# Output pairs in pieces of 6, 12 and 6 slots, with bank changes at the score matmuls

## The chip, the cores and the metric

The kernel runs on one core of a Trainium2 chip. The metric is device time in microseconds (us) of one execution. Below, TensorE is PE, VectorE DVE, ScalarE ACT, GpSimd POOL, and SyncE's DMA queue SP.

## What is computed

For x of 2048 tokens by 576 features, a gated mix of softmax attention (32 heads of 18 features) and an MLP with layer norm (576 to 4608 to 576), all in float32:

```python
def _A_ref(x, wqkv, wo):                 # attention, H = 32, Dh = 18
    q, k, v = qkv[0], qkv[1], qkv[2]
    scores = jnp.einsum("bhqd,bhkd->bhqk", q, k) * scale
    p = _softmax(scores, axis=-1)
    o = jnp.einsum("bhqk,bhkd->bhqd", p, v)
    return (...).reshape(B, S, D) @ wo
def _B_ref(x, w1, b1, w2, b2):
    y = _layernorm(x, axis=-1)
    h = _gelu(jnp.einsum("bsd,df->bsf", y, w1) + b1)
    return jnp.einsum("bsf,fd->bsd", h, w2) + b2
g = _sigmoid((x * gate_w).sum(-1, keepdims=True))
return g * a + (1 - g) * b
```

## The kernel before

Numbers keep float32's precision by being split: a value is a rounded high part plus a low part, and a product is three matmuls (high by high, high by low, low by high).

**The attention loop** (lines 1026 to 1057) has 512 steps: 32 units (a pair of heads, half of the queries) of 16 key chunks. A step has two *score pairs*, `s2` (line 236): two matmuls, one for each head, on row halves 0 to 63 and 64 to 127 of the array. Both write one PSUM tile of two banks, `pss`, of which there is only one, and one exponential on ScalarE (line 238) empties it. So a score pair waits for the exponential of the pair before. In each even step the values' products `pv` (line 253) of two steps follow the first score pair. Two *rounds* a step, `s1_round` (line 195), compute the raw scores of a later unit for their maximum; each is two matmuls with a reduction on DVE for each (line 197), and they share three PSUM banks, so the second matmul of a round reuses the bank of the first matmul of the round before.

**The MLP** fills the time between score pairs. `mlp` is a generator; `fill` takes one piece from it, up to the next cut. It is called three times in two steps: after the even step (share 0), between the two score pairs of the odd step (share 1) and after the odd step (share 2). So two steps make a period with four intervals between score pairs: the first holds `pv`, the others the pieces of share 0, 1 and 2. The MLP's unit of work is a *slot*: two matmuls side by side, one on each row half.

- `h_pair` (line 433): two hidden tiles of 128 by 512, 27 slots of 512 columns. ScalarE then adds the bias (Identity), squares and takes a Tanh (lines 454, 486, 484); GpSimd does the GELU's other steps and the split. It takes one period with pieces of 9 slots, or two with 4, 5, 5 and 4, 5, 4.
- `out_pair` (line 513): 128 tokens by 576 outputs of four hidden tiles, 24 slots of 288 columns: four tiles, in the order `ORDER = (0, 1, 3, 2)`, three products each, and two turns. In turn 0 row half h writes bank h; in turn 1 it writes the other bank. The two halves must not write one bank at a time, so a drain of TensorE stands between the turns (line 502), after 12 slots. Pieces end after 7 and 15 slots. DVE then adds both banks to the sum (line 522).

A group of hidden tiles (36 of them) is an `h_pair` over two periods, four output pairs of one period each, and an `h_pair` over one period: seven periods, 14 steps. The order of every engine's queue is fixed by this program; waits between engines are semaphores. In the first nine groups the MLP's weights are also split: ScalarE copies the high part (line 349), GpSimd subtracts (through line 154), and `ready` (line 366) does that at once when a matmul needs a weight that is not yet prepared.

Of the kernel before, what the change touches and what calls it, by code (L numbers as in the profile page):

```python
# [27 lines left out]
G = 4  # L28
NFC = F // P
NG = NFC // G  # L30
ND = 288
SCALE = DH ** -0.5
GC1 = 0.7978845608028654 * 0.044715
GC0 = 1.0 / 0.044715
LN_EPS = 1e-5
# [23 lines left out]
def gated_mix_kernel(ctx: ExitStack, tc: tile.TileContext, x, wqkv, wo, w1, b1, w2, b2, gate_w, out):  # L59
# [121 lines left out]
        nc.sync.dma_start(VT[pair % 2], v_scr[:, :, pair, :].rearrange("k p e -> p k e"))  # L181

    M4 = {}

    def s1_round(u, r):


        t, kb = (r % 8, r // 8) if u == 0 else divmod(r, 4)
        if r == 0:
            M4[u] = asm.tile([P, 2, 8, 4], F32, name="m4")  # L190
        qa, ka = QA[u % 3], KA[u // 2 % 2]
        for h in range(2):
            r0 = 64 * h
            ps = psum(ps_s1)
            nc.tensor.matmul(ps, qa[r0:r0 + 54, t * P:(t + 1) * P], ka[r0:r0 + 54, kb * TB:(kb + 1) * TB],  # L195
                             start=True, stop=True)
            nc.vector.tensor_reduce(M4[u][:, h, t, kb:kb + 1], ps, axis=AX.X, op=ALU.max)  # L197

# [29 lines left out]
    def s2(u, kc, qb):  # L228
        qa, ka = QA[u % 3], KA[u // 2 % 2]
        n = u * NT + kc  # L230
        if n < 2 and qb == 0:
            RING.insert(n, pp.tile([P, 2, 2, TB], F32, name="p"))
        ps = ps_s2.tile([P, 2, TB], F32, name="pss")
        for h in range(2):
            r0 = 64 * h
            nc.tensor.matmul(ps[:, h, :], ka[r0:r0 + 56, kc * P:(kc + 1) * P], qa[r0:r0 + 56, qb * TB:(qb + 1) * TB],  # L236
                             start=True, stop=True)
        nc.scalar.activation(RING[n % 3][:, qb], ps, AF.Exp, scale=SCALE)  # L238

# [60 lines left out]
    def mlp():  # L300
# [190 lines left out]
        def out_pair(i, t, acc):  # L491

            tb, g = seq[i]
            tok = slice(t * P, (t + 1) * P)
            cs = [slice(nn * ND, (nn + 1) * ND) for nn in range(2)]
            ps = [psum(ps_w) for _ in range(2)]
            ends = {7, 15} if piece[0] == 0 else cuts(24, (3, 2, 1)[piece[0]])
            k = 0
            for turn in range(2):
                if turn == 1:  # L500

                    nc.tensor.drain()
                for j in ORDER:
                    while (i, j) not in HT:
                        cut[0] = 3
                        yield 0
                    hh, hl = HT[i, j]
                    w_ = ready(W2, (i * (G // 2) + j // 2, j % 2))
                    for h_, p_ in ((hh, 0), (hh, 1), (hl, 0)):
                        for h in (0, 1) if turn == 0 else (1, 0):  # L510
                            r = slice(64 * h, 64 * h + 64)
                            nn = h ^ turn
                            nc.tensor.matmul(ps[nn][:, :ND], h_[r, tok], w_[p_][r, cs[nn]],  # L513
                                             start=(k == 0), stop=(k == 6 * G - 1))
                        k += 1
                        if k < 6 * G:
                            if k in ends:
                                cut[0] = 1
                            yield 131
            for nn in range(2):  # L520
                dst = acc[:, t, cs[nn]]
                nc.vector.scalar_tensor_tensor(dst, ps[nn][:, :ND], 0.5, b2b[:, cs[nn]] if g == 0 else dst,  # L522
                                               op0=ALU.mult, op1=ALU.add)
            if g == NG - 1:
                tt = tb * 4 + t
                nc.gpsimd.tensor_scalar(acc[:, t, :], acc[:, t, :], gate1[:, tt:tt + 1], 1.0, op0=ALU.mult, op1=ALU.mult)
                defer(12 if tb < NB - 1 else 4, lambda: nc.sync.dma_start(b_scr[tt * P:(tt + 1) * P, :], acc[:, t, :]))
            cut[0] = 2
            yield 131
# [496 lines left out]
    for u in range(NU):  # L1026
        for kc in range(NT):
            step = u * NT + kc
            if kc == 1:
                if u + 2 < NU:  # L1030
                    load_q(u + 2)
                if u % 2 == 0 and u // 2 + 1 < NPAIR:
                    load_k(u // 2 + 1)
                    load_v(u // 2 + 1)
            if step in (NSTEP - NT, NSTEP - NT + 1, NSTEP - NT + 2, NSTEP - NORM):
                assert hidden[0] == NB - 1
                next(proj)


            next_round()  # L1040
            s2(u, kc, 0)
            run_due(462.0)
            if kc % 2:
                fill(step, 1)
            elif step > 0:
                pv(step - 2)
                while ROWS:
                    ROWS.pop(0)()
                run_due(2080.0)
            if kc % 2:  # L1050
                next_round()
            s2(u, kc, 1)
            if kc % 2 == 0:

                next_round()
            run_due(462.0)
            fill(step, 2 if kc % 2 else 0)
    pv(NSTEP - 2)
# [29 lines left out]
```

## Time and profile before

| | |
|---|---|
| runs, us | 2430.2, 2429.12, 2428.8 (median 2429.12) |
| span of the profiled execution, us | 2421.7 |
| chain that ended last | PE 87%, DVE 3%, issue 3%, POOL 2%, DMA 2%, ACT 2% |
| L513 output pairs, share of that chain | 20% |
| L253, L433, L236, L195, shares of that chain | 19%, 17%, 12%, 10% |
| DMA, mean GB/s | 136 |

The profile shows one execution from its first to its last instruction; of that execution it gives the span alone, and the runs' times include what lies around it. A row of the timeline has the start, the length of a merged run of equal instructions, the engine, the line, the tiles, the shapes and the count; in brackets stands the idle time of the engine before it and what ended that. PEld are TensorE's weight loads, which run ahead of its matmuls. A row of the waits has who waited for whom, the sum in us, how many times and the longest. A row of stretches has the busy time and the count of instructions for PE, PEld, DVE, ACT and POOL, then the granted TensorE clock (1.00 is full), the DMA share and GB/s.

### The profile page before, as it was taken

Reading aid. Unit: us, or ns where it says so; the run is one execution under the profiler, and the core shown is the slowest. Engines: PE = TensorE matmul, PEld = TensorE weight load, DVE = VectorE, ACT = ScalarE, POOL = GpSimd, SP = SyncE. Lnnn points to the kernel's source line nnn. Section 1 sums busy time; section 2 is a strip of 40 time slices with the busy share of each in tenths; the row PEclk is TensorE's granted clock in tenths of the full one; section 3 lists DMA queues with packets and bytes.
Section 4 is the critical chain, followed back from the end, with each engine's and each line's share of the span. In section 5 each row is a group of like instructions: output and inputs, shape, how many; then the busy total and the mean of one; then the engine's idle time right before and its main releaser. Section 6 shows DMA issues by size and latency. Waiting matters only on the chain.

```text
span 2421.7 us, 50623 instructions
## 1 busy us (share of the span) xinstructions
PE 2331.6 (96%) x20585; PEld 1622.0 (67%) x20585; DVE 1652.3 (68%) x2890; ACT 1364.2 (56%) x1604; POOL 965.2 (40%) x964
## 2 busy tenths in 40 slices
PE   8998899998999999999999999999999999999978
PEld 7876556665666666666666666666666666666638
DVE  4665566666667777777777777777777777777415
ACT  4222566655656666666665666666655566666551
POOL 3001565555555444433343444444344334444400
PEclk9999999999999999999999999999999999999979
DMA  7647944434356443333254423242354243232146
GB/s 235 234 150 208 266 143 116 155 113 134 126 159 161 144 149 97 109 103 104 88 157 156 152 95 116 92 133 92 114 160 149 92 144 112 86 120 85 61 144 205
DMA packets 164639, 330.40 MB, mean 136 GB/s; under 512 B 57742, under 2 KB 84402, under 8 KB 153570
## 3 DMA queue, kind: packets, MB, share of 16 engines
q1 hardware_dynamic: 161414, 321.71, 42.5%
q10 hardware_dynamic: 2992, 5.46, 0.6%
q8 instruction: 162, 2.65, 0.5%
q14 instruction: 71, 0.58, 0.1%
HBM read 234.31 MB, written 96.73 MB: 137 GB/s over the span
## 4 chain that ended last, share of the span: by engine, by line
PE 87%; DVE 3%; issue 3%; POOL 2%; DMA 2%; ACT 2%; SPq 0%; ACTq 0%; POOLq 0%; DVEq 0%
PE ps L513 20%; PE ps L253 19%; PE ps L433 17%; PE pss L236 12%; PE ps L195 10%; PE ps L749 4%; PE ps L767 2%; PE ps L988 2%; POOL zz L154 1%; ACT p L238 1%; DVE m L197 1%; DMA big<-y_scr 1%; POOL w L154 1%; PE ps L673 1%; DVE p L733 0%
## 5 line engine op out<-in xcount | busy, mean ns | idle before, releaser
L197 DVE TENSOR_REDUCE m<-ps 128x1 f32<-128x512 f32 x2048 | 1298.5, 684 | 478.1 <-PE ps L195 477.2
L238 ACT ACTIVATE p<-pss 128x1024 f32<-128x1024 f32 x684 | 701.6, 1026 | 507.0 <-PE pss L236 495.2
L513 PE MATMUL ps<-w,hh 64*128 64x288 f32 x4352 | 506.4, 303 | 37.0 <-POOL w L154 20.8
L154 POOL TENSOR_SCALAR zz<-zz 128x512 f32<-128x512 f32 x288 | 178.7, 621 | 872.6 <-ACT zz L486 726.5
L433 PE MATMUL ps<-big,w 64*128 64x512 f32 x3888 | 517.3, 392 | 4.4 <-DMA big<-y_scr 4.3
L236 PE MATMUL pss<-qa,ka 56*128 56x512 f32 x2048 | 483.0, 439 | 20.7 <-ACT p L238 12.3
L238 ACT ACTIVATE ring<-pss 128x1024 f32<-128x1024 f32 x340 | 348.7, 1026 | 248.9 <-PE pss L236 244.3
L513 PEld LDWEIGHTS ps<-w,hh 64*128 64x128 f32 x4352 | 404.6, 189 | 99.0 <-issue 46.1
L195 PE MATMUL ps<-ka,qa 54*128 54x512 f32 x2048 | 458.9, 411 | 7.3 <-DVE m L197 3.6
L433 PEld LDWEIGHTS ps<-big,w 64*128 64x128 f32 x3888 | 389.0, 185 | 73.1 <-DMA big<-y_scr 5.7
L236 PEld LDWEIGHTS pss<-qa,ka 56*128 56x128 f32 x2048 | 199.5, 187 | 275.4 <-ACT p L238 125.6
L154 POOL TENSOR_TENSOR zz<-zz,z 128x512 f32<-128x512 f32 x288 | 371.4, 1290 | 24.0
L513 PE MATMUL ps<-w,hl 64*128 64x288 f32 x2176 | 352.9, 296 | 0.0
L253 PE MATMUL ps<-p,vt 128*32 128x512 f32 x2736 | 348.6, 604 | 0.0
L195 PEld LDWEIGHTS ps<-ka,qa 54*128 54x128 f32 x2048 | 239.4, 186 | 38.8 <-DVE m L197 14.0
L513 PEld LDWEIGHTS ps<-w,hl 64*128 64x128 f32 x2176 | 237.6, 189 | 0.3 <-POOL hl L154 0.2
L154 POOL TENSOR_TENSOR w<-x,w 128x576 fp32r<-128x576 f32 (+1 forms) x54 | 98.2, 1835 | 332.3 <-ACT w L349 308.0
L154 POOL TENSOR_TENSOR hl<-zz,hh 128x512 fp32r<-128x512 f32 x136 | 177.0, 1301 | 11.4
L253 PE MATMUL ps<-ring,vt 128*32 128x512 f32 x1360 | 181.3, 605 | 0.0
L253 PEld LDWEIGHTS ps<-p,vt 128*32 128x32 f32 x2736 | 71.9, 110 | 151.6 <-issue 150.4
L522 DVE SCALAR_TENSOR_TENSOR x<-ps,x 128x288 f32<-128x288 f32 x256 | 105.0, 452 | 38.3 <-PE ps L513 25.9
L749 PE MATMUL ps<-big,wqk 128*128 128x512 f32 x504 | 127.0, 406 | 0.9 <-DVE wqk L667 0.7
(93 smaller groups left out, 1341.8 us busy)
## 6 DMA issues: line engine op xcount, KB each, us to landing
w<-w_scr SPq DMA_DIRECT2D x54, 1152.0 KB
w<-w_scr SPq DMA_DIRECT2D x108, 576.0 KB
x<-in_B_w_dram SPq DMA_DIRECT2D x72, 288.0 KB
w_scr<-w SPq DMA_DIRECT2D x18, 1152.0 KB
w_scr<-w SPq DMA_DIRECT2D x36, 576.0 KB
big<-y_scr SPq DMA_DIRECT2D x42, 384.0 KB
qa<-qk_scr SPq DMA_DIRECT2D x192, 72.0 KB
ka<-qk_scr SPq DMA_DIRECT2D x90, 144.0 KB
```

The lines of the kernel that those rows point to most:

```text
L154: fn(*args, **kw)
L195: nc.tensor.matmul(ps, qa[r0:r0 + 54, t * P:(t + 1) * P], ka[r0:r0 + 54, kb * TB:(kb + 1) * TB], start=True, stop=True)
L197: nc.vector.tensor_reduce(M4[u][:, h, t, kb:kb + 1], ps, axis=AX.X, op=ALU.max)
L236: nc.tensor.matmul(ps[:, h, :], ka[r0:r0 + 56, kc * P:(kc + 1) * P], qa[r0:r0 + 56, qb * TB:(qb + 1) * TB], start=True, stop=True)
L238: nc.scalar.activation(RING[n % 3][:, qb], ps, AF.Exp, scale=SCALE)
L253: nc.tensor.matmul(OB[u][r:r + 32, :], v[:, k, 19 * h:19 * h + 32], RING[c % 3][:, qb, h, :], start=(k == 0), stop=(k == NT - 1))
L433: nc.tensor.matmul(ps[h], wt[w_][r, c, :], Y[s_][r, c, :], start=(k == 0), stop=(k == 26))
L513: nc.tensor.matmul(ps[nn][:, :ND], h_[r, tok], w_[p_][r, cs[nn]], start=(k == 0), stop=(k == 6 * G - 1))
L522: nc.vector.scalar_tensor_tensor(dst, ps[nn][:, :ND], 0.5, b2b[:, cs[nn]] if g == 0 else dst, op0=ALU.mult, op1=ALU.add)
L749: nc.tensor.matmul(ps, w_[:, c, ms], big[:, s_, :], start=(k == 0), stop=(k == len(prods) - 1))
L767: nc.tensor.matmul(ps[:, :ND], big[:, s_, tok], w_[:, c, cs], start=(k == 0), stop=False)
L988: nc.tensor.matmul(ps[:, :ND], OT[b][2][:, s_, tok], w_part(w_, c)[:, cs], start=(k == 0), stop=(k == 13))
```

## The change

An output pair that starts in a piece of share 0 is cut into three parts: 6 slots of turn 0 (the first two tiles), all 12 of turn 1, then the other 6 of turn 0. Each part is one piece, so a bank change falls on the place between two pieces, where score matmuls stand. A pair that starts elsewhere has 12 and 12. Where score matmuls were issued since the last slot, the drain is replaced by an order: an instruction without work on ScalarE waits for the part's last matmul, and the next part's first matmul waits for that instruction. Where none were issued, the drain stays. In the odd step the round ahead of the second score pair now follows it, as in the even step.

```diff
     def s1_round(u, r):
...
+        parted[0] += 1
         for h in range(2):
...
         ps = ps_s2.tile([P, 2, TB], F32, name="pss")
+        parted[0] += 1
...
-            ends = {7, 15} if piece[0] == 0 else cuts(24, (3, 2, 1)[piece[0]])
+            prods = [(j, s_, p_) for j in ORDER for s_, p_ in ((0, 0), (0, 1), (1, 0))]
+            if piece[0] == 0:
+
+                parts = (prods[:6], 0), (prods, 1), (prods[6:], 0)
+            else:
+                parts = (prods, 0), (prods, 1)
             k = 0
-            for turn in range(2):
-                if turn == 1:
+            for place, (part, turn) in enumerate(parts):
+                fresh = place and parted[0] > since
+                if place and not fresh:
 
                     nc.tensor.drain()
-                for j in ORDER:
+                for x_, (j, s_, p_) in enumerate(part):
                     while (i, j) not in HT:
                         cut[0] = 3
                         yield 0
-                    hh, hl = HT[i, j]
+                    h_ = HT[i, j][s_]
                     w_ = ready(W2, (i * (G // 2) + j // 2, j % 2))
-                    for h_, p_ in ((hh, 0), (hh, 1), (hl, 0)):
...
+                    for h in range(2):
+                        r = slice(64 * h, 64 * h + 64)
+                        nn = h ^ turn
+                        mm = nc.tensor.matmul(ps[nn][:, :ND], h_[r, tok], w_[p_][r, cs[nn]],
+                                              start=(k == 0), stop=(k == 6 * G - 1))
+                        if fresh:
+                            tc.add_manual_dep(mm.ins, told.ins.name, SYNC, reason="other rows' bank")
+                            fresh = False
+                    since = parted[0]
+                    if place < len(parts) - 1 and x_ + 1 == len(part):
+                        told = nc.scalar.nop()
+                        tc.add_manual_dep(told.ins, mm.ins.name, SYNC, reason="this row's last")
+                    k += 1
+                    if k < 6 * G:
+                        if x_ + 1 == len(part) and piece[0] < 2:
+                            cut[0] = 1
+                        yield 131
...
-            if kc % 2:
-                next_round()
             s2(u, kc, 1)
-            if kc % 2 == 0:
-
-                next_round()
+            next_round()
             run_due(462.0)
```

TensorE's order in a regular period of an output pair, before, from the round ahead of the odd step's first score pair to its second score pair (L195 is a round, L236 a score pair, L513 slots; `hh` and `hl` are the hidden tile's high and low parts; two matmuls are a slot; drains are not listed):

```order
L195 MATMUL ps<-ka_107,qa_104 128x512 [waits DVE_49] x2
L236 MATMUL pss<-qa_105,ka_106 128x512 [waits Activation_49]
L236 MATMUL pss<-qa_105,ka_106 128x512
L513 MATMUL ps<-w_20123,hh 128x288 x2
L513 MATMUL ps<-w_20123,hl 128x288 x2
L513 MATMUL ps<-w_20121,hh 128x288 x4
L513 MATMUL ps<-w_20121,hl 128x288 x2
L513 MATMUL ps<-w_20117,hh 128x288 x4
L513 MATMUL ps<-w_20117,hl 128x288 x2
L195 MATMUL ps<-ka_107,qa_104 128x512 [waits DVE_49] x2
L236 MATMUL pss<-qa_105,ka_106 128x512 [waits Activation_49]
L236 MATMUL pss<-qa_105,ka_106 128x512
```

The same place after the change, from the part of 12 slots to the round behind the second score pair (lines have moved: L198 is a round, L240 a score pair, L522 slots):

```order
L522 MATMUL ps<-w_20210,hh 128x288 [waits Activation_sequencer_49]
L522 MATMUL ps<-w_20210,hh 128x288 x3
L522 MATMUL ps<-w_20210,hl 128x288 x2
L522 MATMUL ps<-w_20212,hh 128x288 x4
L522 MATMUL ps<-w_20212,hl 128x288 x2
L522 MATMUL ps<-w_20216,hh 128x288 x4
L522 MATMUL ps<-w_20216,hl 128x288 x2
L522 MATMUL ps<-w_20214,hh 128x288 x4
L522 MATMUL ps<-w_20214,hl 128x288 x2
L240 MATMUL pss<-qa_105,ka_106 128x512 [waits Activation_49]
L240 MATMUL pss<-qa_105,ka_106 128x512
L198 MATMUL ps<-ka_107,qa_104 128x512 [waits DVE_49] x2
```

The middle piece has grown from 8 slots to 12 and starts with a wait for ScalarE's instruction, as the last piece, which follows these rows, does too; the round has moved behind the score pair. There are 285 such waits in the program, and two of its drains are left.

TensorE's order in a period of hidden tiles with pieces of 4, 5 and 5 slots, before, from the odd step's first score pair on (L433 are the slots):

```order
L236 MATMUL pss<-qa_105,ka_106 128x512 [waits Activation_49]
L236 MATMUL pss<-qa_105,ka_106 128x512
L433 MATMUL ps<-big,w_19482 128x512 x10
L195 MATMUL ps<-ka_106,qa_103 128x512 [waits DVE_49] x2
L236 MATMUL pss<-qa_105,ka_106 128x512 [waits Activation_49]
L236 MATMUL pss<-qa_105,ka_106 128x512
L433 MATMUL ps<-big,w_19482 128x512 x10
L195 MATMUL ps<-ka_106,qa_103 128x512 [waits DVE_49] x2
```

And after the change (L437 are the slots):

```order
L240 MATMUL pss<-qa_105,ka_106 128x512 [waits Activation_49]
L240 MATMUL pss<-qa_105,ka_106 128x512
L437 MATMUL ps<-big,w_19571 128x512 x10
L240 MATMUL pss<-qa_105,ka_106 128x512 [waits Activation_49]
L240 MATMUL pss<-qa_105,ka_106 128x512
L198 MATMUL ps<-ka_106,qa_103 128x512 [waits DVE_49] x2
L437 MATMUL ps<-big,w_19571 128x512 x10
L198 MATMUL ps<-ka_106,qa_103 128x512 [waits DVE_49] x2
```

The piece between the two score pairs now has no round with it, and the last piece has one on either side.

ScalarE's order in the first output period of a group, before, from the exponential of the even step's second score pair on (L238 is the exponential, L484 the Tanh):

```order
L238 ACTIVATE ring_2352<-pss 128x1024 [waits PE_49]
L238 ACTIVATE p<-pss 128x1024 [waits PE_49]
L484 ACTIVATE zz<-zz 128x512 [waits Pool_49]
L238 ACTIVATE p<-pss 128x1024 [waits PE_49]
L484 ACTIVATE zz<-zz 128x512 [waits Pool_49]
```

And after the change (L242 and L488; the instruction without work has no row of its own, and its wait is shown with the row behind it):

```order
L242 ACTIVATE ring_2352<-pss 128x1024 [waits PE_49]
L242 ACTIVATE p<-pss 128x1024 [waits PE_49]
L488 ACTIVATE zz<-zz 128x512 [waits PE_49,Pool_49]
L242 ACTIVATE p<-pss 128x1024 [waits PE_49]
L488 ACTIVATE zz<-zz 128x512 [waits Pool_49]
```

The first Tanh now stands behind the wait for the last of the 12 slots. There are 32 such Tanh rows.

More of the change, by code (lines that the diff above doesn't have):

```diff
@@ L32 @@
 SCALE = DH ** -0.5
+SYNC = mybir.DependencyInfo(mybir.DependencyClass.Sync, mybir.DependencyReason.DATA)
 GC1 = 0.7978845608028654 * 0.044715
@@ L183, in gated_mix_kernel @@
     M4 = {}
+    parted = [0]
     def s1_round(u, r):
@@ L506, in out_pair @@
                         yield 0
-                    hh, hl = HT[i, j]
+                    h_ = HT[i, j][s_]
                     w_ = ready(W2, (i * (G // 2) + j // 2, j % 2))
-                    for h_, p_ in ((hh, 0), (hh, 1), (hl, 0)):
[L510 to L519, printed above, removed]
+                    for h in range(2):
[15 more added lines that the diff above has]
+                        yield 131
             for nn in range(2):
```

## The prediction

> **What bounds the kernel now.** I read the page first, then the waits, then the timeline of a few stretches, then the busy time by stretch.
>
> ```profile
> PE 2331.6 (96%) x20585; PEld 1622.0 (67%) x20585; DVE 1652.3 (68%) x2890; ACT 1364.2 (56%) x1604; POOL 965.2 (40%) x964
> L502 PEldq DRAIN  x144: 428/1195/1803, 301.4 to 2301.8; - x144
> PEld ps L513 <- issue: 46.1, 145, 0.6
> PEld pss L236 <- ACT p L238: 125.6, 211, 1.7
> L513 PE MATMUL ps<-w,hh 64*128 64x288 f32 x4352 | 506.4, 303 | 37.0 <-POOL w L154 20.8
> ```
>
> TensorE (PE) is the bound on average. All 144 drains ran, and the weight loads of L513 stood still for 46.1 us behind them ("issue", 0.32 us each). That is the most that can go. But the next two rows say that TensorE also waits for others: the score matmuls L236 for ScalarE's exponential, which must empty their only PSUM tile, and L513 for GpSimd. So I look at what each stretch waits for. One regular period of two steps, with an output pair in it:
>
> ```profile
> 1023.10 0.50 PE L236 MATMUL pss<-qa,ka 56*128 56x512 f32 x2
> 1023.43 0.40 PE L195 MATMUL ps<-ka,qa 54*128 54x512 f32 x2
> 1023.86 2.48 DVE L197 TENSOR_REDUCE m<-ps 128x1 f32<-128x512 f32 x4 [0.98 <-PE ps L195]
> 1024.60 0.51 PE L195 MATMUL ps<-ka,qa 54*128 54x512 f32 x2
> 1024.84 0.51 PE L236 MATMUL pss<-qa,ka 56*128 56x512 f32 x2
> 1025.07 0.41 PE L513 MATMUL ps<-w,hh 64*128 64x288 f32 x2
> 1025.44 1.02 ACT L238 ACTIVATE ring<-pss 128x1024 f32<-128x1024 f32 x1 [0.78 <-PE pss L236]
> 1025.60 0.41 PE L513 MATMUL ps<-w,hl 64*128 64x288 f32 x2
> 1026.08 0.30 PEld L513 LDWEIGHTS ps<-w,hh 64*128 64x128 f32 x4 [0.31 <-issue]
> 1026.82 0.40 PE L236 MATMUL pss<-qa,ka 56*128 56x512 f32 x2
> 1027.05 0.44 PE L513 MATMUL ps<-w,hh 64*128 64x288 f32 x4
> 1027.32 1.03 ACT L238 ACTIVATE ring<-pss 128x1024 f32<-128x1024 f32 x1 [0.86 <-PE pss L236]
> 1028.24 0.42 PE L195 MATMUL ps<-ka,qa 54*128 54x512 f32 x2
> 1028.40 0.19 PEld L236 LDWEIGHTS pss<-qa,ka 56*128 56x128 f32 x2
> 1028.47 0.43 PE L236 MATMUL pss<-qa,ka 56*128 56x512 f32 x2
> ```
>
> Unit prices: nine slots run from 1027.05 to 1028.24, 0.132 us each; a round (L195) or a score pair takes about 0.24. At the drain the slots start 0.48 apart (1025.60, 1026.08) instead of 0.13. **The limit of the score pairs**: pair, exponential, next pair. The exponential that starts at 1027.32 ends at 1028.35; the next pair's weights load 0.05 later. From pair to pair that is 1.65 us and already the length of the last interval (1026.82 to 1028.47), so TensorE work taken out of that interval gains nothing. In the first interval (1023.10 to 1024.84) a second limit holds: the second round reuses a bank that the reduction from 1023.86 must first free, and its late half makes rows of 0.51 where others have 0.40: the two row halves then start 0.11 apart.
>
> **The change part by part.** (a) Regular output pairs. Pieces of 7, 8 and 9 slots become 6, 12 and 6, and the last round of the odd step moves behind its second score pair. First interval: one slot less, but its end hangs on reduction and exponential, so it stays. Middle interval: no drain and no round, but four slots more. The first slot starts at 1025.07; twelve of 0.132 put the score pair at 1026.65. Its halves are still 0.11 apart, since no drain lines them up: it ends at 1026.65 + 0.51 = 1027.16, and the exponential starts 0.10 later (as 1026.82 + 0.40 = 1027.22 to 1027.32), at 1027.26 instead of 1027.32. Last interval: round, six slots, round are 0.24 + 0.79 + 0.24 = 1.27 and fit below the limit, which ends it. So 0.06 us of the drain's 0.35 is left; the rest becomes waiting for the exponential. 144 pairs less the two kinds below (32 and 6) are 106: **-6.4 us**.
>
> Two drains stay, where no score matmul came between.
>
> (b) The order through ScalarE. At 285 changes a matmul waits for an instruction on ScalarE that waits for the part's last matmul. No row shows one. A release takes 0.10 from TensorE to ScalarE (above) and 0.05 back (1028.35 to 1028.40). The last slot before the late change starts at 1026.65 - 0.13, its second half 0.11 later, and ends 0.30 after that (page's mean for L513), at 1026.93; the order is then back at 1027.08, while pair and round hold TensorE until 1027.12. I take nothing. From below, nothing excludes it being free; from above, 0.2 us late is still hidden by the exponential's limit; what is later costs in full, 143 times.
>
> (c) What is queued behind that instruction on ScalarE. In 32 periods the next one is a Tanh (L484) of the MLP, before the next exponential:
>
> ```profile
> 1017.26 0.51 PE L236 MATMUL pss<-qa,ka 56*128 56x512 f32 x2
> 1017.49 0.42 PE L513 MATMUL ps<-w,hh 64*128 64x288 f32 x2
> 1018.73 0.62 ACT L484 ACTIVATE zz<-zz 128x512 f32<-128x512 f32 x1
> 1019.69 1.03 ACT L238 ACTIVATE p<-pss 128x1024 f32<-128x1024 f32 x1 [0.34 <-PE pss L236]
> 1020.92 0.40 PE L236 MATMUL pss<-qa,ka 56*128 56x512 f32 x2
> ```
>
> Now the Tanh runs at 1018.73, while TensorE does its slots. Behind the order it starts when the twelfth slot has ended: 1017.49 + 11 x 0.132 + 0.11 + 0.30 = 1019.35, plus 0.10: 1019.45. The exponential starts 0.52 behind a Tanh (0.62 less the 0.10 by which such rows overlap), 1019.97 instead of 1019.69. It ends at 1021.00, the weights load at 1021.05, and a pair that waited so streams 0.1 later, at 1021.15 instead of 1020.92. With rounding 0.25 x 32: **+8.0 us**.
>
> (d) The moved round, in hidden-layer periods with pieces of 4, 5 and 5 slots:
>
> ```profile
> 1057.82 0.51 PE L236 MATMUL pss<-qa,ka 56*128 56x512 f32 x2
> 1058.05 1.44 PE L433 MATMUL ps<-big,w 64*128 64x512 f32 x10
> 1059.22 0.52 PE L195 MATMUL ps<-ka,qa 54*128 54x512 f32 x2
> 1059.44 0.19 PEld L236 LDWEIGHTS pss<-qa,ka 56*128 56x128 f32 x2 [0.15 <-ACT p L238]
> 1059.45 0.51 PE L236 MATMUL pss<-qa,ka 56*128 56x512 f32 x2
> 1061.17 0.44 PE L236 MATMUL pss<-qa,ka 56*128 56x512 f32 x2
> 1068.89 0.19 PEld L236 LDWEIGHTS pss<-qa,ka 56*128 56x128 f32 x2 [0.44 <-ACT p L238]
> ```
>
> The round at 1059.22 fills the wait for the exponential. Behind the pair it no longer does: the pair still starts at 1059.45, and the round's 0.24 is added to an interval whose five slots already reach 1061.17. 0.235 x 28 (36 groups less the first eight, where ScalarE copies weights as well and the interval is longer than TensorE's work): **+6.6 us**. In the period with 4, 5 and 4 slots the last interval has 0.44 of waiting (1068.89), which hides the round: 0 to 0.08 each, taken as 0.03 x 29: **+1**. With nine slots a piece every interval is longer than the limit: nothing.
>
> (e) Six early groups, where GpSimd prepares the third hidden tile's output weights too late:
>
> ```profile
> 489.90 0.61 PE L513 MATMUL ps<-w,hh 64*128 64x288 f32 x2 [3.86 <-POOL w L154]
> 490.31 0.44 PE L513 MATMUL ps<-w,hl 64*128 64x288 f32 x2
> 492.86 0.63 PE L236 MATMUL pss<-qa,ka 56*128 56x512 f32 x2
> 495.65 0.40 PE L236 MATMUL pss<-qa,ka 56*128 56x512 f32 x2
> 485.00:490.00 5.00, 0.97 (x8) 0.56 (x8) 1.29 (x2) 1.04 (x2) 4.59 (x5) 0.85 0.30 99
> 490.00:493.00 3.00, 2.91 (x20) 2.48 (x22) 0.00 (x0) 0.00 (x0) 0.00 (x0) 0.50 0.71 229
> ```
>
> Now 7 slots are done when this wait begins; after the change 13 are, since the same tile comes later in the order. GpSimd's own order is unchanged, so it still ends at 489.90. From there 5 slots remain in the piece: 0.41 + 4 x 0.24 (the slow clock's pace) gives the score pair at 491.27, then round, six slots, round at 0.43, 1.44, 0.43 plus the pair's 0.43: the next pair at 494.00 instead of 495.65. Where the clock recovers sooner it is about 1.0. I take 1.2 x 6 (20.8 / 3.86 is about that many): **-7.2 us**.
>
> Sum: -6.4 + 8.0 + 6.6 + 1 - 7.2 = +2.0, on a span of 2421.7. The runs' median is 2429.12, 7.4 more, which lies around the span and which nothing here touches: **2431 us**.
>
> **The rivals.** *The clock stays up in (e)*, faster. The last column but two of the stretch rows is the granted clock: 0.50 after 3.9 us of waiting. After the change that wait falls apart into about 1.2 and 2.8 us with a slot between. If that keeps full clock, the 11 slots save another 1.2 us and the three round and pair steps 0.6: 1.8 x 6 = 11, 2420. For it: the wait gets shorter; against: 0.97 us of work in 5 us dropped it, and it would be hardly more. The Trainium skill ("TensorE: Matmul & The Clock Gate", Part 1) says that the clock halves after at least one idle window of about 3.4 us; by that the parted wait would keep it. The trace agrees that 3.9 us lowers it, and shows no wait of 2.8 us.
>
> *The drain's time comes back in full*, faster: 0.35 less the 0.11 by which the halves stay apart is 0.24, times 142 is 34 us: 2395. It needs the exponential not to limit; the 1.65 us interval speaks against it.
>
> *The order comes late*, slower: at the late change it finds ScalarE busy with an Identity, Square or weight copy of 0.6 to 0.7, or the release is longer than 0.15. From 0.2 us of lateness it costs; at 0.3 it costs 0.1 x 143 = 14: 2445. Against: the exponential has mostly ended by then.
>
> *GpSimd takes (e) back*, slower: if it is the bound in those groups, the next wait grows by what was won: 2431 + 7 = 2438. Against: it is 40% busy and idles behind each of these waits.
>
> *The change doesn't do it*: the waits might fall away in the build. 285 stand in the order, so hardly: 2429.
>
> **How the numbers follow.** A measurement of this kernel can tell about 0.2% from no change, 4.9 us: 2424.3 to 2434.0. Forecast 0.55 (own range 2424 to 2437: inside 0.44, below 0.05, above 0.06); clock stays 0.15; drain in full 0.06; order late 0.12; GpSimd 0.10; nothing done 0.02. Faster 0.05 + 0.15 + 0.06 = 0.26, same 0.44 + 0.02 = 0.46, slower 0.06 + 0.12 + 0.10 = 0.28. The range 2414 to 2446 takes in all but the drain in full and an order later than 0.3 us.
>
> **What would show it.** (a) Exponentials of output periods still 1.65 to 1.8 us apart, and more idle of L236's weight loads behind them than the 125.6 us. (b) No idle at the changes' matmuls put down to ScalarE. (c) Tanh rows that start after the twelfth slot. (d) The pair after five slots alone, then 0.24 more to the next. (e) L513's 20.8 us behind GpSimd smaller, and the granted clock there. It is wrong if the middle interval's halves line up again (a gains to 0.17 a period), or if any change's matmul waits over 0.2 us.

## The result and the profile after

| | median, us | range, us | runs |
|---|---|---|---|
| before | 2430.23 | 2425.02 to 2432.14 | 20 |
| after | 2433.86 | 2430.43 to 2436.08 | 20 |

The ratio is 1.0019, with a 95% interval of 1.0013 to 1.0025: about 4.6 us longer (3.2 to 6.1; the medians are 3.6 apart). That is inside the 0.2% that the prediction called no change, and 2.9 us above its 2431. The drains are gone, and the time is not shorter. The profiled executions differ by more, 2421.7 and 2432.7 us; how much of those 11 us is the change's own is counted further below.

From the page of the kernel after, the engines' busy time and the slots' group (busy time, mean ns of one; then the idle time before them and what ended most of it):

```profile
PE 2352.6 (97%) x20585; PEld 1638.7 (67%) x20585; DVE 1639.8 (67%) x2890; ACT 1364.5 (56%) x1604; POOL 964.7 (40%) x964
...
L522 PE MATMUL ps<-w,hh 64*128 64x288 f32 x4352 | 482.0, 295 | 18.5 <-POOL w L155 12.3
```

From its waits (who waits for whom, sum, times, longest):

```profile
PEld pss L240 <- ACT p L242: 130.7, 189, 1.8
...
ACT zz L488 <- PE ps L522: 17.5, 27, 0.7
...
PE ps L522 <- POOL w L155: 12.3, 6, 2.6
...
PEld ps L522 <- issue: 1.9, 3, 1.2
```

The stalls behind drains fell from 46.1 to 1.9 us, and the slots' wait for GpSimd from 20.8 to 12.3. Against that, the score pairs' weight loads (L240) wait 130.7 us for the exponential instead of 125.6, the Tanh (L488) now waits for slots, and TensorE is busy 21 us longer with the same 20585 matmuls. The timeline of a regular output period, from score pair to score pair, shows where the time of the drain is now:

```profile
1024.68 0.50 PE L240 MATMUL pss<-qa,ka 56*128 56x512 f32 x2
...
1026.96 0.50 PE L240 MATMUL pss<-qa,ka 56*128 56x512 f32 x2
...
1028.65 0.56 PE L240 MATMUL pss<-qa,ka 56*128 56x512 f32 x2
...
1028.98 0.50 PE L522 MATMUL ps<-w,hh 64*128 64x288 f32 x4
...
1029.31 1.03 ACT L242 ACTIVATE p<-pss 128x1024 f32<-128x1024 f32 x1 [0.71 <-PE pss L240]
...
1030.58 0.44 PE L240 MATMUL pss<-qa,ka 56*128 56x512 f32 x2
...
1031.12 1.02 ACT L242 ACTIVATE p<-pss 128x1024 f32<-128x1024 f32 x1 [0.79 <-PE pss L240]
...
1032.20 0.54 PE L240 MATMUL pss<-qa,ka 56*128 56x512 f32 x2
```

The length of a merged row doesn't tell how far its two halves are apart. By their single records, the halves of the pairs of 1028.65 and 1032.20 start 0.17 and 0.14 us apart; those of 1026.96 start 0.00 apart, and each of them takes 0.50 instead of 0.39.

The intervals are 2.28, 1.69, 1.93 and 1.62 us. The third holds twelve slots and no drain, and is about as long as the one with eight slots, a round and a drain was (1.98). The fourth holds a round, six slots and a round, and ends where the exponential lets it: 1031.12 + 1.02 = 1032.14, and the pair follows at 1032.20. Long interval full, short interval waiting: that is where the drain's time went.

The same four intervals over the whole trace, as medians of the starts of the score pairs, by kind of period (some 30 to 40 periods a row, each kernel's one profiled execution; kernels other than before and after are those of the experiments). Rows without a kind are of the kind of the row above:

| kernel, kind of period | 1 | 2 | 3 | 4 | period, us |
|---|---|---|---|---|---|
| before, second output pair of a group | 2.201 | 1.739 | 1.981 | 1.657 | 7.582 |
| after | 2.287 | 1.622 | 1.935 | 1.697 | 7.544 |
| drain_alone | 2.186 | 1.738 | 1.685 | 1.760 | 7.376 |
| pieces_alone | 2.283 | 1.621 | 1.922 | 1.716 | 7.541 |
| rounds_alone | 2.194 | 1.734 | 1.754 | 1.936 | 7.619 |
| round_at_change | 2.195 | 1.736 | 1.778 | 1.675 | 7.387 |
| round_then_drain | 2.203 | 1.737 | 2.072 | 1.654 | 7.671 |
| before, first output pair (with Tanh) | 2.285 | 1.738 | 1.986 | 1.661 | 7.667 |
| after | 2.285 | 1.622 | 1.937 | 2.001 | 7.846 |
| pieces_alone | 2.289 | 1.622 | 1.924 | 1.656 | 7.488 |
| tanh_first | 2.284 | 1.623 | 1.937 | 1.629 | 7.484 |
| before, hidden pair 4, 5, 5 | 2.174 | 1.751 | 1.637 | 1.725 | 7.287 |
| after | 2.174 | 1.751 | 1.621 | 1.971 | 7.520 |
| hidden_rounds | 2.174 | 1.751 | 1.637 | 1.726 | 7.288 |

### The profile page after: what moved, and what is told of

It is laid out like the page before. It is cut to its first block, busy times and chain, and to the rows that moved or that the text cites. A ratio compares the mean times of both kernels' runs of the same rounds, so it can differ in the third digit from the quotient of the medians.

```text
span 2432.7 us, 50768 instructions
## 1 busy us (share of the span) xinstructions
PE 2352.6 (97%) x20585; PEld 1638.7 (67%) x20585; DVE 1639.8 (67%) x2890; ACT 1364.5 (56%) x1604; POOL 964.7 (40%) x964
## 4 chain that ended last, share of the span: by engine, by line
PE 85%; DVE 4%; ACT 4%; DMA 3%; issue 2%; POOL 2%; SPq 0%; ACTq 0%; POOLq 0%; DVEq 0%
PE ps L257 19%; PE ps L437 17%; PE ps L522 17%; PE pss L240 12%; PE ps L198 11%; PE ps L765 4%; PE ps L783 2%; DMA big<-y_scr 2%; ACT p L242 1%; PE ps L1004 1%; DVE m L200 1%; POOL zz L155 1%; ACT ring L242 1%; ACT zz L488 1%; PE ps L689 1%
## 5 line engine op out<-in xcount | busy, mean ns | idle before, releaser
L242 ACT ACTIVATE p<-pss 128x1024 f32<-128x1024 f32 x684 | 700.5, 1024 | 487.7 <-PE pss L240 473.2
L240 PE MATMUL pss<-qa,ka 56*128 56x512 f32 x2048 | 519.8, 451 | 25.8 <-ACT p L242 13.1
L198 PE MATMUL ps<-ka,qa 54*128 54x512 f32 x2048 | 522.0, 420 | 10.2 <-DVE m L200 6.4
L437 PE MATMUL ps<-big,w 64*128 64x512 f32 x3888 | 522.3, 394 | 2.5 <-DMA big<-y_scr 2.5
L522 PE MATMUL ps<-w,hh 64*128 64x288 f32 x4352 | 482.0, 295 | 18.5 <-POOL w L155 12.3
L242 ACT ACTIVATE ring<-pss 128x1024 f32<-128x1024 f32 x340 | 348.2, 1024 | 246.2 <-PE pss L240 239.6
L522 PEld LDWEIGHTS ps<-w,hh 64*128 64x128 f32 x4352 | 435.4, 187 | 43.9 <-POOL w L155 13.6
L437 PEld LDWEIGHTS ps<-big,w 64*128 64x128 f32 x3888 | 393.7, 186 | 73.1 <-DMA big<-y_scr 3.2
L240 PEld LDWEIGHTS pss<-qa,ka 56*128 56x128 f32 x2048 | 213.1, 186 | 282.0 <-ACT p L242 130.7
L522 PE MATMUL ps<-w,hl 64*128 64x288 f32 x2176 | 393.3, 294 | 0.0
L257 PE MATMUL ps<-p,vt 128*32 128x512 f32 x2736 | 350.9, 608 | 0.0
L198 PEld LDWEIGHTS ps<-ka,qa 54*128 54x128 f32 x2048 | 284.0, 187 | 69.8 <-DVE m L200 21.5
L522 PEld LDWEIGHTS ps<-w,hl 64*128 64x128 f32 x2176 | 280.4, 186 | 0.0
L257 PE MATMUL ps<-ring,vt 128*32 128x512 f32 x1360 | 182.0, 607 | 0.0
L257 PEld LDWEIGHTS ps<-p,vt 128*32 128x32 f32 x2736 | 72.2, 110 | 156.8 <-issue 155.6
```

Source lines behind the costliest of these rows:

```text
L257: nc.tensor.matmul(OB[u][r:r + 32, :], v[:, k, 19 * h:19 * h + 32], RING[c % 3][:, qb, h, :], start=(k == 0), stop=(k == NT - 1))
L437: nc.tensor.matmul(ps[h], wt[w_][r, c, :], Y[s_][r, c, :], start=(k == 0), stop=(k == 26))
L522: mm = nc.tensor.matmul(ps[nn][:, :ND], h_[r, tok], w_[p_][r, cs[nn]], start=(k == 0), stop=(k == 6 * G - 1))
```

## The experiments

The theory: the removed drains are worth some 30 us, and three things of the change eat them, namely the pieces of 6, 12 and 6 slots, the Tanh behind the order's instruction, and the moved round where it had covered a wait. A gain in the early groups comes on top. The rivals: the score pairs' limit lets no drain be worth anything, or the order through ScalarE costs what the drain did. Ratios are to the kernel before, run on the same chip (its medians: 2429.43 with drain_alone, pieces_alone, rounds_alone and hidden_rounds; 2427.77 with tanh_first, both, round_at_change and early_groups; 2427.53 with round_then_drain and combined).

**drain_alone.** The kernel before, without the drain and without the bank change; pieces of 7, 8 and 9 stay.

```diff
-                if turn == 1:
-                    nc.tensor.drain()
...
-                        for h in (0, 1) if turn == 0 else (1, 0):
+                        for h in (0, 1):
-                            nn = h ^ turn
+                            nn = h
```

> The kernel before without its drains and without the bank change (both turns write the same bank from the same row half, so half of each output product's columns are left out); pieces of 7, 8 and 9 slots and the rounds stay. If the gain of the changed kernel went into its 6, 12, 6 pieces: the middle interval of an output period falls from 1.98 to about 1.74 us, the others stay, 138 x 0.24 = 33 us less, ratio to before about 0.986. If the exponential already hid the drain: under 10 us less, ratio over 0.996.

Measured: 2398.14 us, ratio 0.9870 (0.9856 to 0.9883). The drain, with the bank change that it stands for, is worth 31 us where the pieces are balanced. The score pairs around the former change:

```profile
1021.07 0.51 PE L236 MATMUL pss<-qa,ka 56*128 56x512 f32 x2
...
1022.75 0.19 PEld L236 LDWEIGHTS pss<-qa,ka 56*128 56x128 f32 x2 [0.21 <-ACT p L238]
1022.75 0.50 PE L236 MATMUL pss<-qa,ka 56*128 56x512 f32 x2
...
1024.52 0.41 PE L236 MATMUL pss<-qa,ka 56*128 56x512 f32 x2
```

The third interval shrinks to 1.68 and just reaches the exponential's limit (0.21 of waiting), the fourth is 1.77. That the limit makes the drain worthless falls, and so does the 1.65 us argument of the prediction as one against any gain: it held for the interval behind the drain, while the one with the drain had 0.3 us above it.

**pieces_alone.** The kernel after, without bank change, drain and order; its pieces and moved rounds stay.

```diff
-                fresh = place and parted[0] > since
-                if place and not fresh:
-                    nc.tensor.drain()
+                fresh = False
...
-                        nn = h ^ turn
+                        nn = h
...
-                    if place < len(parts) - 1 and x_ + 1 == len(part):
-                        told = nc.scalar.nop()
-                        tc.add_manual_dep(told.ins, mm.ins.name, SYNC, reason="this row's last")
```

> The changed kernel with pieces of 6, 12 and 6 slots, but without bank change, drain and order through ScalarE (both turns write the same bank, so half of each output product's columns are left out). If the order costs only the 32 Tanh rows behind it: 32 x 0.18 = 6 us below the changed kernel, about 2428, ratio to before about 0.9995, and output periods without a Tanh stay at 7.54 us. If the order is late at the bank changes: 14 us or more below the changed kernel, ratio 0.996 or less.

Measured: 2419.72 us, ratio 0.9958 (0.9946 to 0.9971), 14.1 us below the median of the kernel after and 21.6 above drain_alone, which also has neither drain nor order. What lies between is the pieces and the moved round, less the gain of the early groups. A regular period is 7.541 us with these pieces, 7.376 with the old ones: some 0.16, of which 0.10 lies in the first interval and 0.19 in the third and fourth together, less 0.12 in the second. With the order it is 7.544, so in regular periods the order costs nothing. In periods with a Tanh it is 7.488 without and 7.846 with the order. So the 14 us are about those of the expectation's second case, but not for its reason: the order is not late at the bank changes, the Tanh behind it costs twice what was expected, 0.36 instead of 0.18. From the loop's second period to its last score pair, put side by side, pieces_alone is 12.2 us ahead of the kernel after; in the 32 first output pairs behind the early groups it gains 11.2. Its whole profiled execution is 14.8 shorter; 2.7 of that lies before the first score pair, where nothing was edited.

**rounds_alone.** The kernel before with the round moved and nothing else.

```diff
-            if kc % 2:
-                next_round()
             s2(u, kc, 1)
-            if kc % 2 == 0:
-                next_round()
+            next_round()
```

> The kernel before, in which only the odd step's last round moves behind the second score pair; drains and pieces stay. If the moved round loses its cover in the 4, 5, 5 periods: 28 x 0.23 + 29 x 0.045 = 8 us slower, ratio about 1.003, the 4, 5, 5 period at 7.52 instead of 7.29 us. If a round costs the same wherever it stands: no change.

Measured: 2440.07 us, ratio 1.0042 (1.0028 to 1.0056), a loss of 10 us. The 4, 5, 5 periods grow by 0.23, output periods by 0.04 (7.582 to 7.619). In two output periods at the end of a unit, which are 8.02 and 7.89 us in the kernel before, it takes 9.28 and 9.21; the kernel after has 8.81 and 8.97 there. In the traces of all the kernels the two take 8.8 to 9.3 us where the round of the period ahead was moved behind the pair, and 7.8 to 8.0 where it was not. The rows of the first of them in the kernel after, and then the round's second weight load in the kernel before:

```profile
734.11 1.27 DVE L211 TENSOR_TENSOR nm<-nm,nmh 128x16 f32<-128x16 f32 x1
...
736.76 0.18 PEld L198 LDWEIGHTS ps<-ka,qa 54*128 54x128 f32 x1 [0.78 <-DVE m L200]
737.36 0.18 PEld L198 LDWEIGHTS ps<-ka,qa 54*128 54x128 f32 x1 [0.41 <-DVE m L200]
```

```profile
745.08 0.18 PEld L195 LDWEIGHTS ps<-ka,qa 54*128 54x128 f32 x1 [0.28 <-DVE m L197]
```

Read from these rows: the unit's last round comes later, so the last step of its maximum on DVE (L211) does too, and the next round's weights wait 0.78 and 0.41 us for reductions, where they waited 0.28 before. No run separates this from other things that the later round moves.

**hidden_rounds.** The kernel after, with the round ahead of the second score pair where a hidden pair fills the step.

```diff
+            early = kc % 2 and hidden_piece[0]
+            if early:
+                next_round()
             s2(u, kc, 1)
-            next_round()
+            if not early:
+                next_round()
```

> The changed kernel, but in hidden-layer periods the odd step's last round stands ahead of the second score pair as before; output periods keep the changed order. If the moved round costs what the two traces show: 8 us below the changed kernel, about 2426, ratio to before about 0.9985, with the 4, 5, 5 period back at 7.29 us. If not: as the changed kernel, ratio 1.002.

Measured: 2425.61 us, ratio 0.9981 (0.9971 to 0.9990); the 4, 5, 5 periods are back at 7.288. The kernel after shows the cost that this takes away, in a view of TensorE alone:

```profile
1054.04 0.50 PE L240 MATMUL pss<-qa,ka 56*128 56x512 f32 x2
1054.28 1.43 PE L437 MATMUL ps<-big,w 64*128 64x512 f32 x10
1055.66 0.50 PE L240 MATMUL pss<-qa,ka 56*128 56x512 f32 x2
1056.00 0.39 PE L198 MATMUL ps<-ka,qa 54*128 54x512 f32 x2
1056.23 1.32 PE L437 MATMUL ps<-big,w 64*128 64x512 f32 x10
1057.39 0.39 PE L198 MATMUL ps<-ka,qa 54*128 54x512 f32 x2
1057.62 0.39 PE L240 MATMUL pss<-qa,ka 56*128 56x512 f32 x2
```

Pair to pair is 1.62 us with five slots alone, the exponential's limit, and then 1.96 with a round more: 0.23 longer for the two than before (1.63 and 1.72).

**tanh_first.** The kernel after, with the order's instruction put on ScalarE's queue behind what `run_due` issues.

```diff
-                        told = nc.scalar.nop()
-                        tc.add_manual_dep(told.ins, mm.ins.name, SYNC, reason="this row's last")
+                        told = []
+                        tell.append((told, mm))
...
             run_due(max(spent[0] - t, GAP))
+            say()
```

> The changed kernel, but the order's instruction is issued on ScalarE behind what comes due at that place, so the 32 Tanh rows stand ahead of it. If the Tanh behind the order is what the first output period loses (7.84 us against 7.545 without an order): 32 x 0.295 = 9.4 us below the changed kernel, about 2424.5, ratio to before about 0.9977, that period at 7.55 us and the bank changes still without a wait. If the order itself is what costs: as the changed kernel, ratio 1.002, or worse, since it now comes later.

Measured: 2423.94 us, ratio 0.9982 (0.9973 to 0.9991). The kernel after, from the twelfth slot of a first output pair on:

```profile
1015.00 0.41 PE L522 MATMUL ps<-w,hl 64*128 64x288 f32 x2
...
1015.13 0.52 PE L240 MATMUL pss<-qa,ka 56*128 56x512 f32 x2
...
1015.54 0.63 ACT L488 ACTIVATE zz<-zz 128x512 f32<-128x512 f32 x1 [0.65 <-PE ps L522]
...
1016.07 1.01 ACT L242 ACTIVATE p<-pss 128x1024 f32<-128x1024 f32 x1
...
1017.13 0.19 PEld L240 LDWEIGHTS pss<-qa,ka 56*128 56x128 f32 x2 [0.40 <-ACT p L242]
```

tanh_first at the same place:

```profile
1011.82 0.62 ACT L495 ACTIVATE zz<-zz 128x512 f32<-128x512 f32 x1
...
1012.17 0.52 PE L247 MATMUL pss<-qa,ka 56*128 56x512 f32 x2
...
1012.73 1.02 ACT L249 ACTIVATE p<-pss 128x1024 f32<-128x1024 f32 x1 [0.28 <-PE pss L247]
...
1013.80 0.18 PEld L247 LDWEIGHTS pss<-qa,ka 56*128 56x128 f32 x2
```

Where the Tanh stands behind the order it starts 0.13 after the last slot's end and the exponential 0.53 later: from pair to pair 2.00 us. Where it stands ahead, it runs under the slots and the interval is 1.63. The period falls to 7.484 us, below the 7.55 of the expectation: 7.545 is the length of the third and fourth pairs' periods without an order, while the first pairs have 7.488 (table). So with the Tanh ahead of it the order costs nothing here either.

**both.** tanh_first and hidden_rounds together.

> tanh_first and hidden_rounds together. If the two losses are separate they add: 9.4 + 8 = 17 us below the changed kernel, about 2417, ratio to before about 0.9945. If they share slack: about as the better of the two, 0.9975.

Measured: 2416.26 us, ratio 0.9948 (0.9934 to 0.9963). Against the kernel after, the first two give 0.37% and 0.38%, both together 0.71%. They are separate costs, and without them the change is a gain.

**round_at_change.** The kernel before with its pieces of 7, 8 and 9; the odd step's last round moves to the bank change, and an order through ScalarE stands in place of the drain (137 of 144 changes).

```diff
-                    nc.tensor.drain()
+                    if piece[0] == 1 and rounds and looped[0]:
+                        told = nc.scalar.nop()
+                        tc.add_manual_dep(told.ins, mm.ins.name, SYNC, reason="turn 0's last")
+                        next_round()
+                        taken[0] = True
+                    else:
+                        nc.tensor.drain()
...
-            if kc % 2:
+            if kc % 2 and not taken[0]:
                 next_round()
```

> The kernel before, pieces of 7, 8 and 9 slots kept, but in the middle piece the odd step's last round moves from the piece's end to the bank change, and the order through ScalarE takes the drain's place there (137 of 144; the rest keep the drain). If the 12 slots in one piece are what ate the drain's gain and a round covers most of the order's way (0.45 us from the last slot's start, against 0.13 + 0.24 of slot and round): the middle interval falls from 1.98 to 1.70 to 1.80 us, 137 x 0.2 = 27 us less, about 2402, ratio about 0.989. If the order's way is longer than a round and a drain's worth: no gain, ratio 1.0.

Measured: 2403.04 us, ratio 0.9899 (0.9884 to 0.9913). TensorE around the change:

```profile
1025.10 0.51 PE L237 MATMUL pss<-qa,ka 56*128 56x512 f32 x2
...
1025.90 0.36 PE L520 MATMUL ps<-w,hl 64*128 64x288 f32 x2
1026.03 0.54 PE L196 MATMUL ps<-ka,qa 54*128 54x512 f32 x2
1026.38 0.53 PE L520 MATMUL ps<-w,hh 64*128 64x288 f32 x4
...
1026.87 0.41 PE L237 MATMUL pss<-qa,ka 56*128 56x512 f32 x2
```

From the last slot before the change to the first after it are 0.48 us, as with the drain, but now a round (L196) stands in them that had to be done anyway. Slot and round alone would be 0.37 (0.13 and 0.24); the other 0.11 is the order's return, for which the next slot's weights stand still 0.12 us here. The third interval is 1.77, the fourth still ends near the exponential's limit.

**round_then_drain.** The same, with a drain behind the round in place of the order.

```diff
-                        told = nc.scalar.nop()
-                        tc.add_manual_dep(told.ins, mm.ins.name, SYNC, reason="turn 0's last")
                         next_round()
                         taken[0] = True
+                        nc.tensor.drain()
```

> As round_at_change, but with a drain behind the moved round in place of the order through ScalarE. If it is the order that turns the round into cover, since a drain must also wait for the round's own matmuls: the drain costs its 0.35 us again behind the round, the middle interval stays near 1.98 us, ratio to before 1.0 (0.998 to 1.003). If the place of the round alone did it: ratio 0.99 as round_at_change.

Measured: 2439.39 us, ratio 1.0047 (1.0034 to 1.0060), 36 us above round_at_change, and above the 1.003 that the expectation went up to. So it is the order that gains, not the round's new place. TensorE there, and then the wait of the slots' weight loads in this kernel:

```profile
1027.59 0.40 PE L519 MATMUL ps<-w,hl 64*128 64x288 f32 x2
1027.72 0.57 PE L196 MATMUL ps<-ka,qa 54*128 54x512 f32 x2
1028.39 0.53 PE L519 MATMUL ps<-w,hh 64*128 64x288 f32 x4
```

```profile
PEld ps L519 <- issue: 61.3, 145, 0.7
```

Round and drain are 0.80 us from slot to slot, and the stalls are 61.3 us where the drain between two slots had 46.1.

**early_groups.** The parts and the order only in the first nine groups, the moved round only in their output periods; the rest as in the kernel before.

```diff
+            if i >= NG and piece[0] == 0:
+                ends = {7, 15}
+            if i >= NG:
+                parts = (prods, 0), (prods, 1)
...
-                fresh = place and parted[0] > since
+                fresh = place and parted[0] > since and i < NG
```

> The changed order of parts, the order through ScalarE and the moved round only in output periods of the first nine groups; all else as before, drains included. If those groups won what the two traces show (10.8 us up to 690 us): about 2419, ratio to before about 0.9955. If GpSimd takes it back later: ratio about 1.0.

Measured: 2418.05 us, ratio 0.9960 (0.9947 to 0.9973). In the output periods of nine groups the change gains about 10 us; the rest of it costs about 14 (0.9960 against 1.0019).

**combined.** round_at_change, with the 6, 12, 6 parts and their order in the first output pair of each of the first nine groups alone.

```diff
+            if piece[0] == 0 and i < NG and t == 0 and rounds and looped[0]:
+                for place, (part, turn) in enumerate(((prods[:6], 0), (prods, 1), (prods[6:], 0))):
...
+            for turn in range(2) if k == 0 else ():
```

> round_at_change, and in the first output period of the first nine groups the changed kernel's 6, 12, 6 with its order and the round behind the score pair. If the gain of the early groups is that of this first period, where GpSimd's weights are late, it adds to round_at_change: 25 + 9 = 34 us, about 2394, ratio to before about 0.986. If it came from all four output periods or shares slack: 0.988 to 0.990.

Measured: 2395.26 us, ratio 0.9867 (0.9852 to 0.9882): 32 us below the kernel before, and as fast as drain_alone. It is the fastest of all.

## Why the prediction came out as it did

The total came out 2.9 us off, and that is partly luck: what (e) gained more than predicted, 5.0 us, is about what (d) left out, 4.9 us.

**(a) Regular output pairs**: the limit that hides the drain's gain was right, and the size held: the periods shrink by 0.04 to 0.07 us (predicted 0.06). But that size is luck in part, since two intervals moved that were taken as fixed and about cancel. The table's second, which is the first that the prediction speaks of, lost 0.05 to 0.12, so it hung on TensorE's slot after all; the table's first, with the products `pv` (L257, before L253), gained 0.09. From the rows of a second output pair in the kernel after, then of one before:

```profile
1017.13 0.50 PE L240 MATMUL pss<-qa,ka 56*128 56x512 f32 x2
1017.57 1.06 PE L257 MATMUL ps<-ring,vt 128*32 128x512 f32 x8
```

```profile
1020.92 0.40 PE L236 MATMUL pss<-qa,ka 56*128 56x512 f32 x2
1021.24 1.07 PE L253 MATMUL ps<-ring,vt 128*32 128x512 f32 x8
```

From the products' start to the next pair are 1.85 us in regular periods of all these kernels; what grows is the way from the pair to the products, 0.43 us instead of 0.32 here. Halves that start apart are not the whole reason: these start 0.00 apart in both rows, and the matmuls of the pair that had to wait (its weights load at 1017.13 too) take 0.50 us instead of 0.40. The first of the twelve slots also starts later behind its pair, by 0.10 in the rows shown (1028.65 to 1028.98, before 1024.84 to 1025.07) and by 0.06 in the medians (0.34 and 0.27), with and without the order.

**(b) The order**: right. No wait of the slots is put down to its return in a regular period, and 7.544 against 7.541 us bounds it. The rival that it comes late falls.

**(c) The Tanh**: right in its rows to 0.03 us, but for the 0.1 from the weights to the pair: both start at 1017.13, and the 0.1 shows in the pair's length. The term was +8.0; against the kernel before it is 0.18 in 32 periods, 5.7, since the second and third intervals gained there too. Against the same pieces without the order it is 0.36, 11.2 in those 32 periods. Against tanh_first they sum to 11.6, of which 9.9 is left between the runs' medians and 9.0 by the ratios.

**(d) The moved round**: 0.233 in 4, 5, 5 periods (predicted 0.235), 0.04 in 4, 5, 4 periods (0.03). Taken as nothing, and wrong: periods with nine slots grow from 10.259 to 10.345 us, by the same first interval behind an output pair as in (a) (2.219 to 2.306), some 3 us in 35 of them, which is not the moved round's (rounds_alone has 10.231, hidden_rounds 10.345) but comes with the new pieces; and the two unit ends above, 1.9 us together.

**(e) The early groups** is the term that was mis-sized: -7.2 predicted; the six periods are 2.48, 0.79, 2.59, 2.61, 1.26 and 2.50 us shorter, 12.2 together. Over the kernels with these parts, the six sum to 74.5 to 77.3 us (75.5 here), over those with the old parts and drains to 87.3 to 88.0, so it is not one execution's chance. The step that failed is the one from the working's 1.65 us down to 1.2; in the group of the working it should have gone up. The kernel after in the group of the prediction's rows, TensorE alone, then its stretches (busy times and counts, granted clock, DMA share, GB/s):

```profile
486.26 0.40 PE L522 MATMUL ps<-w,hh 64*128 64x288 f32 x2 [0.98 <-ACT w L353]
489.17 0.41 PE L522 MATMUL ps<-w,hh 64*128 64x288 f32 x2 [2.52 <-POOL w L155]
...
489.93 0.39 PE L240 MATMUL pss<-qa,ka 56*128 56x512 f32 x2
...
492.41 0.63 PE L240 MATMUL pss<-qa,ka 56*128 56x512 f32 x2
```

```profile
489.00:490.20 1.20, 1.03 (x14) 0.96 (x14) 0.00 (x0) 0.00 (x0) 0.11 (x1) 1.00 0.08 12
490.20:493.00 2.80, 2.80 (x24) 2.09 (x21) 2.06 (x5) 1.54 (x2) 0.92 (x2) 0.50 0.94 312
```

The wait ends 9.22 us after the period's first pair (479.95), before 9.30 (480.60 to 489.90): GpSimd keeps its pace. The parted wait (0.98 and 2.52) then leaves full clock for the five slots and the score pair, and the clock falls to half at 490.2. From the wait's end to the period's end are 3.24 us, before 5.75, and 4.10 by the working. The working had the clock at half at once. In another early group that is so:

```profile
425.50:427.00 1.50, 1.11 (x8) 1.11 (x10) 0.00 (x0) 0.00 (x0) 0.34 (x1) 0.50 1.00 403
```

So *the clock stays up* falls as the rival put it: the clock drops in both, at most one piece later. It drops in all six, and in the last two of them behind waits of only 0.98 and 0.99 us, and 0.98 and 1.03 us (to 0.50 from 613.1 and 674.5 us on). The trace before could have told: one of its six waits is 2.23 us, shorter than the 2.8 that the rival goes by, and half clock follows it too:

```profile
617.81 0.40 PE L513 MATMUL ps<-w,hh 64*128 64x288 f32 x2 [2.23 <-POOL w L154]
618.30:621.60 3.30, 3.21 (x26) 2.69 (x24) 0.92 (x2) 0.46 (x1) 0.00 (x0) 0.50 0.81 263
```

In each trace here all changes of the clock lie whole multiples of 3.41 us apart. On this grid, over the twelve profiled executions and with the matmuls' spans as the profile gives them, half clock followed every stretch at full clock in which matmuls ran less than 0.48 of the 3.41 us, and none in which they ran more than 0.76 of it. So the time of the fall is not set by the wait's end: one such stretch, with 0.40 us of matmuls, ended at 425.36, inside a wait that ended at 425.89; the other, with 1.05 us of matmuls, at 490.22, 1.0 us behind the wait. The Trainium skill ("TensorE: Matmul & The Clock Gate", Part 1) asks for an idle window of about 3.4 us before the clock halves; by that these waits of 0.98 and 2.5 to 2.6 us, with one slot between, would have kept it. The measurement decides against it here: 0.50 behind both. *GpSimd takes it back* falls too: at the end of the sixth such period (690 us) the kernel after is 10.8 us ahead within the loop, all other terms included, and early_groups keeps its gain to the end.

***The drain's time comes back in full***: right in its size (31 us by drain_alone, 34 in the prediction) and wrong for this change. What spoke against it in the prediction, the limit of the last interval, is not what stopped it. Twelve slots in one interval, and in the next one six that wait, did.

**The account.** Of the 11.0 us between the profiled executions, 1.8 lie before the loop's second period (it begins at 268.0 and 269.8), 1.5 of them before the first score pair, where no edit is. Over all kernels here that begin ranges from 266.4 to 269.8. Two periods near 1770 us (8.81 and 7.78 us before; 10.78 and 9.70 after) make 3.9 more; in the other profiles they are 8.2 to 12.0 and 7.8 to 10.2, with and without the moved round, so that is chance. The 5.3 that remain agree with the runs' 4.6 (3.2 to 6.1). In the loop they come from 10.8 ahead at 690 us, 1.9 lost at the two unit ends, and from then on some 29 groups of 0.385 us each by the medians (0.18 with Tanh, -0.04, -0.07 and -0.04 in the other output pairs, 0.23, 0.04 and 0.09 in the hidden pairs), 11.2. That sums to 2.3; some 3 us are left. Summed period by period instead of by medians, most of them stand in other periods about the ends of units, 0.1 to 0.3 us each.

What stays open: why the other unit ends take these 0.1 to 0.3 us; why the executions differ by up to 3.4 us ahead of the loop's second period; and how much of the first interval's 0.09 is due to pairs that wait and how much to halves that start apart, since no run changed one alone.

## What to carry to other kernels

A wait that is removed pays only in an interval that is longer than the next limit, so compare each interval with that limit before cutting work differently: here the unbalanced pieces, with the round moved, cost some 0.16 us a period, in some 137 periods 22 us of the 31 that the drains were worth. What stands behind an instruction that only waits, on the same queue, waits as well; put such an instruction behind the work that is ready. Before work is moved, ask what wait it covers: here the round was worth most when it was moved to stand in the bank change itself.

## What the hardware showed that was not expected

A drain right behind a round costs more than one between slots: 0.42 against 0.32 us of standing weight loads for each (61.3 and 46.1 us, 145 times). A signal from TensorE to ScalarE and back is hidden by one round up to 0.11 us: slots stand 0.48 us apart with a round and the order between, and the same with the drain alone. A score pair that had to wait for the exponential took 0.50 us a matmul instead of 0.40, and the products behind it started 0.1 us later. The granted clock fell to 0.50 after waits of 0.98 and 2.5 to 2.6 us with a slot between, and even after two of about 1 us each; it changed only at multiples of 3.41 us, and behind every stretch of that length with matmuls in less than 0.48 of it.
